# Loading the first expert's rows behind raw weights, splitting its weights without VectorE, and mixing its first products into the last head pair's order

## The chip, the cores and the metric

The kernel runs on one core of one Trainium2 chip. The time is device microseconds from start to end of one execution; a kernel's time is the median of its runs. Engines are called PE (TensorE), DVE (VectorE), ACT (ScalarE), POOL (GpSimd) and SP (SyncE, which here only issues transfers and loads registers). Each engine works through its own instructions in program order.

## The reference

Bucketed attention on 4 batches, 8 heads, 768 tokens and head size 64, and then a mixture of 8 experts on the 3072 tokens:

```
q_bucket, k_bucket = bits of sign(q @ proj), sign(k @ proj)      # 6 bits
scores = q @ k^T / 8, minus 1e9 where the buckets differ
attn   = softmax(scores) @ v                                     # x: 3072 x 512
expert = argmax(x @ w_gate); gate = softmax(x @ w_gate)[expert]
out    = gate * (relu(x_e @ w1[e]) @ w2[e])                      # per expert e
```

## The kernel before, in words

The attention part runs over 16 groups of one pair of heads each. A pair has 12 units (128 rows by 768 keys of one head). The order of each pair's work is written out by hand as a string of words: `HEAD` for the first pair, `PLAN` for the middle ones, `LAST` for the last pair. Every engine receives its instructions in the order in which the words are issued. A word with one or two dashes works for the pair before or the one before that. The words of `LAST` are:

- `S` score products of a unit (PE, L297 and L299), `R` their row minimum (DVE, L307), `X` the exponential (ACT, L313).
- `T` four transposes of the exponentials (PE, L327), `E..a` or `E..v` their copy out of PSUM on ACT (L379) or DVE (L377). `V0` and `V1` are the products with the values for the first and second half of the rows (PE, 24 matmuls, L389), `O` their copy on ACT (L395).
- `K` the product of the attention output with the router's weights and an identity (PE, L409), `L` its scaled copy (DVE, L419). `M` inverts the row sums.
- `n` and `t` are the two halves of one weight part of the first expert: a copy that rounds the raw weights (`nP` on POOL, `nA` on ACT) and the subtraction that leaves the rest (`tP` on POOL, `tV` on DVE, L964). There are 16 parts: 0 to 7 for the first matrix, 8 to 15 for the second. Eight parts are done at such words, the others by `weights` behind an `R` of an odd unit, copy and subtraction both on POOL (L714, L715). Two raw buffers hold two parts each; finishing an odd part issues the next raw load (L704, on SP).
- `r0` and `r1` are single steps of the generator `route_last` (L492) for the two halves of the last batch's last rows. Its first step takes a PSUM tile of the two named `t`, the third step ends with an exponential on ACT (L515), the fourth is a count on PE (L480, L482), the fifth and sixth give the slots and the gate on DVE (L522 to L530). `c0` and `c1` write these rows to DRAM at their slots, three indirect transfers each on POOL (L539).
- `x`, `g`, `h` turn the first expert's rows (transposes on PE L801, copy on ACT L803, rest on DVE L805). They read `XG[0]`, which `rows(0)` loads from DRAM (L744). `m` is one of eight products of the first matrix (12 matmuls on PE, L822), `u` its relu on ACT (L836), `d` the rest on DVE (L838). `m4` to `m7` need parts 4 to 7, `m0` to `m3` parts 0 to 3.

PSUM has two tiles named `t` (used by T, V, K and the routing steps) and three named `s` (used by S, x, m and the second products). A tile can be taken again when its last reader, in program order, is done.

Behind the last word, `rows(1)` loads the second half of the first expert's rows (L744); it reads rows that `c0` and `c1` have written, so it waits on SP for them. Then `rank_all` orders the experts and SP reads seven registers (L601), and only then come the raw loads for the second expert. PE goes on with the two second products of the first rows (48 matmuls, L879); four of the transposes of `rows(1)` stand behind the 44th of them (L784). After that come the first products of the second half, whose relu copies on ACT alternate with the second expert's weight copies.

In the last pair `route_step` writes the first half of an earlier batch's rows at the first three `R` words, and issues `rows(0)` at the third.

Of the kernel before, what the change touches and what calls it, by code (L numbers as in the profile page):

```python
# [31 lines left out]
M0 = float(2 ** 34)  # L32
# [22 lines left out]
def lsh_attention_moe(ctx, tc, qk, qk2, v, proj, wg, w1, w1p, w2, out):  # L55
# [634 lines left out]
    def raw_load(c, a):  # L690

        r, k = divmod(c, 4)
        if k < 2:
            src = (w1p if r else w1)[bass.ds(EV[r], 1)].rearrange("o (a p) f -> p (o a) f", p=128)[:, 2 * a:2 * a + 2,
                                                                                k * 512:(k + 1) * 512]
        else:
            o = (k - 2) * 4 + 2 * a
            src = w2[bass.ds(EV[r], 1)].rearrange("o (a p) d -> p (o a) d", p=128)[:, o:o + 2, :]
        n = 2 * c + a
        if n < 10 or n % 2:  # L700
            t = moe.tile([128, 2, 512], F32, name="raw", bufs=2)
        else:
            t = P2["p"].tile([128, 2, 512], F32, name="raw2", bufs=2)
        nc.sync.dma_start(t, src)  # L704
        RAW[c, a] = t
# [21 lines left out]
    def rows(n):  # L727

        r, o, c = PH[n]
        if n >= 2:  # L730
            b = -(-c // 32)
            x = XB[n] = P2["p"].tile([128, CB, 4 * 32], F32, name="xb")
            for a in range(4):
                nc.sync.dma_start(x[32 * a:32 * a + 32, :b],
                                  xsv[bass.ds(EV[r], 1), o:o + 32 * b, a * PW + E:a * PW + E + 2 * D]
                                  .rearrange("o (b i) w -> i (o b) w", i=32))
            t = len(tiles_of(c))
            XG[n] = P2["p"].tile([128, 4, 2], F32, name="xg", bufs=2)
            nc.sync.dma_start(XG[n][:, :t], xsv[bass.ds(EV[r], 1), o:o + 128 * t, GC:GC + 2]
                              .rearrange("o (j p) w -> p (o j) w", p=128))  # L740
            return
        XG[n] = wk.tile([128, 2, RW], F32, name="xd")
        for j, (i, _) in enumerate(tiles_of(c)):
            nc.sync.dma_start(XG[n][:, j], xsv[bass.ds(EV[r], 1), o + i:o + i + 128].rearrange("o p w -> p (o w)"))  # L744
# [190 lines left out]
    NC = NU // 2  # L935
    routes, parts, pick = {}, list(range(16)), pick_first()

    def weights(n):

        for _ in range(n):  # L940
            k = parts.pop(0)
            chunk_part(k // 4, k % 4)
            h = k // 2 + 2
            if k % 2 and h < 8:
                raw_load(h // 2, h % 2)

    def weight_half(op, x):

        if op == "n":
            k = parts.pop(0)  # L950
            c, a = divmod(k, 4)
            if a == 0:
                CH[c] = moe.tile([128, 2, 4, 512], F32R, name=HOME[c])
            o, i = CH[c][:, 0, a], RAW[c, a // 2][:, a % 2]
            if x == "A":
                nc.scalar.activation(o, i, AF.Copy)
            else:
                nc.gpsimd.tensor_copy(o, i)
            lows.append(k)
        else:  # L960
            k = lows.pop(0)
            c, a = divmod(k, 4)
            w, r = CH[c], RAW[c, a // 2][:, a % 2]
            ENG[x].tensor_tensor(w[:, 1, a], r, w[:, 0, a], op=OP.subtract)  # L964
            h = k // 2 + 2
            if k % 2 and h < 8:
                raw_load(h // 2, h % 2)
# [15 lines left out]
    """.split()  # L983

    LAST = """
        S5 R5 nP T30- E30a- S1 nP T31- E31v- S4 X5 nP T32- E32v- S0 R0 X0 K0-- L0-- R4 X4 tV V1- S8 tP O1- tP R1 X1
        M1- T21 E21v T20 E20a S2 R2 T01 E01a T22 E22a X2 S6 R6 X6 K1- L1- T00 E00v S11 R11 X11 S3 M0- T02 E02v R3 X3
        V0- O0- R8 X8 S10 T11 E11v T10 E10a S7 nP tP S9 M0 T12 R10 E12a X10 V0 R9 X9 O0 T40 E40a T51 E51a T41 E41a T42
        R7 E42a T50 E50a T52 E52v K0 L0 nP tV x0 X7 T31 E31a T30 T32 E30a M1 E32v K0- g0 h0 V1 O1 K1 nP tP nA tP L0-
        r0 r0 r0 r0 r0 r0 c0 x2 g2 h2 m6 u6 m1 u1 L1 r1 r1 r1 r1 r1 d6 r1 c1 d1 m7 u7 d7 m3 u3 d3 m4 u4 d4 m2 u2 d2 m0  # L990
        u0 d0 nP tP m5 u5 d5
    """.split()

    SCAT = {}
# [8 lines left out]
    def route_step(g, w, k):  # L1003

        b, q = divmod(g - NP, NP)
        if 0 <= b < B - 1 and w[0] == "R" and q == 1 and {(g - 2, "L0"), (g - 2, "L1")} <= DONE and steps[b] < 6:
            if b not in routes:
                routes[b] = route(b)
            on(b, 1)
        if 0 <= b < B - 1 and q == 2:  # L1010
            if w == "G":
                on(b, 8 - steps[b])
            elif w[0] == "R" and 8 <= steps[b] < 11:
                on(b, 1)
        s = {7: (0, 0), 8: (0, 1), 11: (1, 0), 12: (1, 1), 14: (2, 0)}.get(g)
        if w == "P7" and s:
            go(scatter(*s), 4)
        if g == NG - 1 and w[0] == "R" and k < 3:
            if k == 0:
                SCAT[0] = scatter(2, 1)  # L1020
            go(SCAT[0], 1)
            if k == 2:
                rows(0)

    def loads(g):

# [26 lines left out]
    def step(g, w):  # L1053

        n = g - w.count("-")
        w = w.rstrip("-")
        if w[0] in "SRXTEVOMKLDGHPBNA":
            z = n, w.rstrip("av")
            if n < 0 or z in DONE:
                return  # L1060
            DONE.add(z)
        op, x = w[0], w[1:]
        if op == "S":
            i = 12 * n + int(x)
            if i % 2 == 0:
                before(i // 2)
            score(i)
        elif op == "R":
            i = 12 * n + int(x)
            peak(i)  # L1070
            behind(i)
        elif op == "X":
            expo(12 * n + int(x))
        elif op == "T":
            trans(6 * n + int(x[0]), int(x[1]))
        elif op == "I":
            loads(n)
        elif op == "D" and n:
            blocks(12 * n + int(x))
        elif op == "E":  # L1080
            trans_ev(6 * n + int(x[0]), int(x[1]), x[2] == "v")
        elif op == "V":
            for kt in range(NT):
                pv(2 * n + int(x[0]), kt)
        elif op == "O":
            pv_end(2 * n + int(x))
        elif op == "M":
            sums(2 * n + int(x))
        elif op == "K":
            TK[2 * n + int(x)] = tok(2 * n + int(x))  # L1090
        elif op == "L":
            tok_ev(2 * n + int(x), TK.pop(2 * n + int(x)))
        elif op == "G" and n + 1 < NG:
            lsh_mm(n + 1)
        elif op == "H" and n + 1 < NG:
            lsh_ev(n + 1)
        elif op == "B" and 0 < n < NG - 1:
            lsh_bits(n + 1)
        elif op == "N" and n + 1 < NG:
            mask(2 * n + 2)  # L1100
            mask(2 * n + 3)
        elif op == "A" and n + 1 < NG:
            if x == "2":
                xk = XL[n + 1][:, S:]
                nc.gpsimd.tensor_scalar(xk, xk, KS, 1.0, op0=OP.mult, op1=OP.mult)
            else:
                upper(2 * n + 2, int(x))
        elif op == "P" and n + 1 < NG:
            split(2 * n + 2 + int(x) // 4, int(x) % 4)
        elif op in "kjqlp":  # L1110
            cut(op, int(x[0]), int(x[1]), x[2])
        elif op == "y":
            lsh_first(int(x[0]), int(x[1]))
        elif op == "b":
            bits_first(int(x[0]), int(x[1]))
        elif op == "f":
            if x == "0":
                before(0)
            score(0, (x == "1",))
        elif op == "i":  # L1120
            if int(x[0]) not in SC:
                SC[int(x[0])] = ps.tile([128, 2, 512], F32, name="s", bufs=3)
            warmth(SC[int(x[0])][:, 0], int(x[1]))
        elif op == "s":
            split(2 + int(x[0]), int(x[1]))
        elif op == "z":
            mask(2 + int(x))
        elif op == "w":
            lsh_bits(1)
        elif op in "xgh":  # L1130
            xt_first(op, int(x))
        elif op == "m":
            mm1(0, int(x))
        elif op in "ud":
            relu(op, int(x))
        elif op == "r":
            go(last[int(x)], 1)
        elif op == "c":
            go(scatter(B - 1, int(x)), 4)
        elif op in "nt":  # L1140
            weight_half(op, x)

    last = [route_last(B - 1, 0), route_last(B - 1, 1)]
    for g in range(NG):
# [146 lines left out]
```

## Time and profile before

| | |
|---|---|
| median of 3 runs | 710.57 us (710.15 to 710.75) |
| the profiled execution | 709.86 us, of which the span is 708.1 us |
| PE busy | 694.2 us, 98% of the span, 4219 matmuls |
| DVE, ACT, POOL busy | 446.7, 433.6, 470.7 us |
| TensorE clock granted, mean | 0.995 of full speed |

The attention part takes the first 400 us, the experts the rest. PE's busy share says how long a matmul was in it, not that it ran at its full rate: a matmul that runs at half clock is twice as long and counts as busy. So the slices of PE's share must be read beside the granted clock.

### The profile page before, as it was taken

The numbers are of one execution on the slowest core, as the hardware profiler recorded it, in microseconds if no ns is written. First come the engines' busy times: TensorE is split into PE (matmuls) and PEld (weight loads), VectorE is DVE, ScalarE is ACT, GpSimd is POOL, SyncE is SP. The second block draws the span as 40 slices with busy tenths as digits, with TensorE's granted clock in tenths as the row PEclk, the third lists the DMA queues.
The fourth block names the chain that finished last, engine by engine and source line by source line (L and its number), as shares of the span: only waits on it lengthen the run. The fifth ranks groups of instructions, "written<-read, shape, count | busy, mean of one in ns | idle before, by whom it ended". The sixth has DMA issues, their size and how long they took to land.

```text
span 708.1 us, 12282 instructions
## 1 busy us (share of the span) xinstructions
PE 694.2 (98%) x4219; PEld 566.5 (80%) x4219; DVE 446.7 (63%) x916; ACT 433.6 (61%) x863; POOL 470.7 (66%) x520
## 2 busy tenths in 40 slices
PE   8999999999999999999999799999999999999997
PEld 5777777776877686867776589899999999989896
DVE  8878787878787778788882533541838533362521
ACT  7988888878888788887865114644344344444320
POOL 7967755695785967867938335765667676768532
PEclk9999999999999999999999899999999999999999
DMA  7519777885977556875693138476446394738101
GB/s 288 151 38 263 202 220 204 245 232 184 272 218 213 160 148 200 223 221 150 197 275 111 68 131 243 164 194 145 157 135 172 123 183 148 194 134 223 70 10 41
DMA packets 64528, 123.09 MB, mean 174 GB/s; under 512 B 15329, under 2 KB 29025, under 8 KB 64400
## 3 DMA queue, kind: packets, MB, share of 16 engines
q1 hardware_dynamic: 56736, 103.17, 51.6%
q0 software_dynamic: 7584, 19.10, 8.5%
q8 instruction: 34, 0.56, 0.4%
q14 instruction: 30, 0.25, 0.1%
q10 hardware_dynamic: 144, 0.02, 0.0%
HBM read 65.75 MB, written 26.33 MB: 130 GB/s over the span
## 4 chain that ended last, share of the span: by engine, by line
PE 90%; issue 4%; POOL 2%; ACT 1%; DVE 1%; DMA 0%; POOLq 0%; ACTq 0%
PE t L389 19%; PE s L822 18%; PE s L859 10%; PE s L297 10%; PE s L299 9%; PE t L327 9%; PE s L879 8%; PE t L409 3%; PE t L254 2%; PE s L888 1%; POOL w L718 1%; PE t L103 1%; POOL w L715 0%; ACT e L313 0%; DMA out_dram<-e,ix 0%
## 5 line engine op out<-in xcount | busy, mean ns | idle before, releaser
L307 DVE TENSOR_SCALAR_CACHE_REDUCE e<-s 128x768 f32<-128x768 f32 x192 | 178.7, 953 | 61.4 <-PE s L299 52.4
L313 ACT ACTIVATE e<-e,m 128x768 f32<-128x768 f32 x192 | 178.0, 930 | 15.2 <-DVE e L307 12.9
L718 POOL TENSOR_TENSOR w<-raw,w 128x512 fp32r<-128x512 f32 x112 | 144.4, 1315 | 38.6 <-ACT w L717 37.9
L389 PE MATMUL t<-pt,vt 128*64 128x384 f32 x768 | 133.7, 499 | 2.8 <-DVE pt L377 2.8
L822 PE MATMUL s<-xh,w 128*128 128x456 f32 (+6 forms) x672 | 126.8, 346 | 0.0
L822 PEld LDWEIGHTS s<-xh,w 128*128 128x128 f32 x672 | 119.2, 188 | 3.0
L389 PEld LDWEIGHTS t<-pt,vt 128*64 128x64 f32 x768 | 53.4, 139 | 68.4 <-issue 63.4
L838 DVE SCALAR_TENSOR_TENSOR hh<-s,hh 128x256 fp32r<-128x256 f32 (+7 forms) x64 | 35.5, 555 | 109.2 <-ACT hh L836 109.1
L327 PE MATMUL t<-ident,e 128*128 128x128 f32 x648 | 92.0, 274 | 1.3 <-DVE pt L377 0.5
L379 ACT ACTIVATE pt<-t 128x512 f32<-128x512 f32 (+1 forms) x148 | 82.3, 581 | 13.7 <-PE t L327 12.3
L836 ACT ACTIVATE hh<-s 128x256 fp32r<-128x256 f32 (+7 forms) x64 | 31.3, 490 | 90.3 <-PE s L822 86.9
L327 PEld LDWEIGHTS t<-ident,e 128*128 128x128 f32 x648 | 76.7, 140 | 8.1 <-ACT pt L379 1.9
L349 DVE STREAM_TRANSPOSE w<-e 128x768 f32<-128x768 f32 x84 | 79.1, 964 | 0.8 <-DMA pt<-w 0.6
L859 PE MATMUL s<-hh,w 128*128 128x456 f32 (+3 forms) x384 | 74.9, 356 | 0.0
L859 PEld LDWEIGHTS s<-hh,w 128*128 128x128 f32 x384 | 71.1, 188 | 2.6
L717 ACT ACTIVATE w<-raw 128x512 fp32r<-128x512 f32 x112 | 66.4, 622 | 3.3 <-DMA raw<-in_w1p_dram 3.3
L895 POOL DMA_INDIRECT out_dram<-y,ix x26 | 25.9, 995 | 62.0 <-DVE y L893 29.4
L879 PE MATMUL s<-w,hh 128*128 128x512 f32 (+1 forms) x240 | 56.4, 394 | 0.0
L297 PE MATMUL s<-w 80*128 80x384 f32 x192 | 55.3, 369 | 0.0
L297 PE MATMUL s<-qk 80*128 80x384 f32 x192 | 54.9, 368 | 0.0
L879 PEld LDWEIGHTS s<-w,hh 128*128 128x128 f32 (+1 forms) x240 | 44.7, 187 | 10.4
L299 PE MATMUL s<-qk 128*128 128x384 f32 x192 | 49.8, 341 | 0.0
(219 smaller groups left out, 987.1 us busy)
## 6 DMA issues: line engine op xcount, KB each, us to landing
pt<-w SPq DMA_DIRECT2D x224, 144.0 KB, 3.7
raw<-in_w_dram SPq DMA_DIRECT2D x36, 512.0 KB, 3.4
raw<-in_w1p_dram SPq DMA_DIRECT2D x28, 512.0 KB, 3.3
xd<-in_qk_dram SPq DMA_DIRECT2D x14, 768.0 KB, 7.7
sorted_rows<-xr SPq DMA_DIRECT2D x6, 1156.0 KB, 7.8
vt<-in_v_dram SPq DMA_DIRECT2D x16, 384.0 KB, 3.4
masks<-bits POOLq DMA_DIRECT2D x14, 192.0 KB, 4.0
sorted_rows<-sorted_rows SPq DMA_DIRECT2D x2, 1156.0 KB, 6.1
```

Source lines behind the costliest of these rows:

```text
L297: nc.tensor.matmul(p[:, a, :HALF], k[0:80, 2, c], k[0:80, 3, n], start=i >= 4, stop=i < 4)
L299: nc.tensor.matmul(p[:, a, :HALF], k[:, 0, c], k[:, 1, n], start=i < 4, stop=i >= 4)
L307: nc.vector.tensor_scalar(e, SC.pop(i)[:, :, :HALF], CEIL, None, op0=OP.min, op1=OP.min, accum_out=m)
L313: nc.scalar.activation(e, e, AF.Exp, bias=m, scale=-1.0, accum_out=SM[g, hf][:, t, s:s + 1])
L327: nc.tensor.transpose(o[:, j, w], e[w][:, kt // 3, (kt % 3) * 128:(kt % 3) * 128 + 128], ident)
L349: nc.vector.transpose(z[:, :, c, w].rearrange("p g (k i) -> p g k i", i=32), e)
L379: nc.scalar.activation(o, x, AF.Copy)
L389: nc.tensor.matmul(p[s * 64:(s + 1) * 64, :HALF], VT[g][:, kt, s, :], PT[u][:, :, :, s, kt].rearrange("p a t i -> p t a i"), start=(kt == ...
L718: nc.gpsimd.tensor_tensor(w[:, 1, a], r, w[:, 0, a], op=OP.subtract)
L822: nc.tensor.matmul(p[:, :c], w[:, a, d, fs], x[:, b, d, :c], start=(k == 0), stop=(k == 11))
L859: nc.tensor.matmul(p[:, :c], w[:, a, f % 4, ms], h[b][:, f, :c], start=(k == 0), stop=(k == 23))
L879: nc.tensor.matmul(p[:pw], HH[n][b][:, f, i:i + pw], w[:, a, f % 4], start=(k == 0), stop=(k == 23))
```

## The change

Four edits. `rows(0)` is no longer issued at the third `R` word but as soon as four of the sixteen parts have been taken (behind the raw load that this part issues). No weight part has its subtraction on DVE or its copy on ACT any more; nine parts go through `nP` and `tP`. The order of the words of `LAST` is another: of the eight products `m` of the first expert three stand between the transposes of the last pair, one between them and `V1`, one between `V1` and `K1`, and three behind that; `x2`, `x0` come ahead of the last scores. And eviction copies have changed engines here and there.

```
+    def rows_asked():
+        if len(parts) <= 12 and 0 not in XG:
+            rows(0)
 ...
             if k % 2 and h < 8:
                 raw_load(h // 2, h % 2)
+            rows_asked()
 ...
     LAST = """
-        S5 R5 nP T30- E30a- S1 nP T31- E31v- S4 X5 nP T32- E32v- S0 R0 X0 K0-- L0-- R4 X4 tV V1- S8 tP O1- tP R1 X1
-        M1- T21 E21v T20 E20a S2 R2 T01 E01a T22 E22a X2 S6 R6 X6 K1- L1- T00 E00v S11 R11 X11 S3 M0- T02 E02v R3 X3
-        V0- O0- R8 X8 S10 T11 E11v T10 E10a S7 nP tP S9 M0 T12 R10 E12a X10 V0 R9 X9 O0 T40 E40a T51 E51a T41 E41a T42
-        R7 E42a T50 E50a T52 E52v K0 L0 nP tV x0 X7 T31 E31a T30 T32 E30a M1 E32v K0- g0 h0 V1 O1 K1 nP tP nA tP L0-
-        r0 r0 r0 r0 r0 r0 c0 x2 g2 h2 m6 u6 m1 u1 L1 r1 r1 r1 r1 r1 d6 r1 c1 d1 m7 u7 d7 m3 u3 d3 m4 u4 d4 m2 u2 d2 m0
-        u0 d0 nP tP m5 u5 d5
+        S5 nP tP R5 T31- E31a- S1 T30- E30v- S0 R0 X5 T32- E32a- K0-- L0-- X0 S8 R8 X8 nP tP M1- R1 X1 V1- O1- S4 R4
+        T00 E00a T01 E01v S6 T02 E02v R6 S3 R3 X4 T21 E21a T20 E20a S2 S11 X6 T22 R2 X2 E22a R11 V0- O0- x2 g2 h2 x0
+        g0 h0 K1- L1- S7 S9 X3 M0 T11 T10 E11a E10v M0- S10 nP tP X11 K0- L0- nP tP nP tP nP tP nP tP nP tP T12 R10 R9
+        E12a V0 X9 X10 T51 O0 T50 m4 E50v T52 R7 E51a T40 u4 d4 m7 E52a E40a T41 E41v T42 E42v m5 X7 M1 T31 E31a T30
+        E30a T32 K0 L0 r0 r0 r0 u5 d5 m2 u7 d7 E32a V1 O1 u2 d2 m3 u3 d3 r0 K1 L1 r1 r1 r1 r0 r0 c0 m1 u1 d1 m0 u0 d0
+        m6 u6 d6 r1 r1 r1 c1
     """.split()
 ...
             go(SCAT[0], 1)
-            if k == 2:
-                rows(0)
 ...
             weight_half(op, x)
+            if op == "t":
+                rows_asked()
```

## Rows read from the trace of the kernel before

**Rows 1.** Chain that ended last, in order of time: start us, us, engine, tile, line, count.

```profile
365.77 0.73 PE t L409 x6
368.80 4.09 PE t L389 x24
373.79 0.87 PE t L327 x8
376.51 4.04 PE t L389 x24
405.34 8.73 PE s L822 x72
414.07 10.26 PE s L879 x44
```

**Rows 2.** Timeline of PE: start us, us, line, operation, count [idle before <-releaser].

```profile
380.47 4.00 PE L327 MATMUL t<-ident,e 128*128 128x128 f32 x24
391.32 6.92 PE L389 MATMUL t<-pt,vt 128*64 128x384 f32 x24 [2.77 <-DVE pt L377]
398.89 1.00 PE L409 MATMUL t<-wgt,ot 128*128 128x144 f32 x6 [0.65 <-ACT ot L395]
424.17 0.60 PE L784 MATMUL t<-ident,xd 128*128 128x128 f32 x4
```

**Rows 3.** Stretches of 2 us: busy time by engine, granted clock, DMA share, GB/s.

```profile
388.00:390.00 2.00, 0.55 (x5) 0.33 (x3) 0.66 (x1) 0.00 (x0) 1.92 (x4) 1.00 0.05 15
390.00:392.00 2.00, 0.68 (x2) 0.29 (x4) 1.97 (x6) 0.00 (x0) 1.52 (x1) 0.56 0.71 247
392.00:394.00 2.00, 2.00 (x10) 0.78 (x8) 0.38 (x1) 0.00 (x0) 0.00 (x0) 0.50 0.00 0
396.00:398.00 2.00, 2.00 (x12) 0.61 (x8) 0.00 (x0) 0.00 (x0) 0.00 (x0) 0.73 0.00 0
```

**Rows 4.** Timeline of DVE, the same columns.

```profile
389.34 1.06 DVE L964 TENSOR_TENSOR w<-raw,w 128x512 fp32r<-128x512 f32 x1 [3.19 <-POOL w L958]
390.61 0.65 DVE L377 COPY pt<-t 128x512 f32<-128x512 f32 x1
400.95 0.17 DVE L522 TENSOR_TENSOR pb<-t,pb 128x8 f32<-128x8 f32 x1 [0.36 <-PE t L482]
401.90 0.18 DVE L530 RECIPROCAL xr<-rf 128x3 f32<-128x3 f32 x1
402.67 0.60 DVE L419 TENSOR_TENSOR xr<-t,r 128x432 f32<-128x432 f32 x1
404.86 0.18 DVE L514 TENSOR_TENSOR rl<-t,rf 128x24 f32<-128x24 f32 x1
```

**Rows 5.** Timeline of ACT, the same columns.

```profile
387.38 0.60 ACT L803 ACTIVATE xhe<-s 128x512 fp32r<-128x512 f32 x1
400.62 0.22 ACT L515 ACTIVATE ex<-rl 128x24 f32<-128x24 f32 x1 [1.26 <-DVE rl L514]
```

**Rows 6.** Timeline of POOL, the same columns.

```profile
402.85 1.01 POOL L539 DMA_INDIRECT sorted_rows<-xr,slot  x1 [2.00 <-issue]
410.05 0.96 POOL L539 DMA_INDIRECT sorted_rows<-xr,slot  x1 [0.21 <-issue]
```

**Rows 7.** Timeline of SP's issues, the same columns; `x16` spans sixteen issues.

```profile
353.60 12.55 SPq L355 DMA_DIRECT2D pt<-w  x16
366.65 0.90 SPq L744 DMA_DIRECT2D xd<-sorted_rows  x2
413.74 0.90 SPq L744 DMA_DIRECT2D xd<-sorted_rows  x2
421.58 8.57 SPq L704 DMA_DIRECT2D raw<-in_w1p_dram  x3
```

**Rows 8.** Issues of the DMA view: KB each, median us from issue to landing.

```profile
pt<-w SPq DMA_DIRECT2D x224, 144.0 KB, 3.7
xd<-sorted_rows SPq DMA_DIRECT2D x4, 289.0 KB, 2.7
```

## The prediction

> **What bounds the kernel now.** PE is busy 98% of the span, so I looked for the stretch where it isn't, or where it isn't at full rate. Three views, in this order. The chain of waits, read for what one step costs when nothing holds it: `K` 0.73 us, eight transposes (two `T`) 0.87, a `V` 4.04, 72 of the 96 matmuls of the first expert's `m` 8.73 [rows 1]. Then PE's timeline over the end of the last pair, where the same steps cost more: six `T` take 4.00 us instead of 2.61, `V1` starts 2.77 us after PE has gone idle and then takes 6.92, and the last `K1` waits 0.65 [rows 2]. Then the granted clock in stretches of 2 us: 1.00 through the idle time, falling within 390 to 392, 0.50 until between 396 and 398 [rows 3]. `V1` ran at the lower level of 1.2 GHz, which cost 6.95 - 4.04 = 2.9 us [rows 1, 2].
>
> Why `V1` waited is in DVE's timeline: the eviction of the last transposes (L377 at 390.61) stood behind a weight subtraction (L964) that had held DVE for 3.19 us, because POOL had not made that part's copy [rows 4].
>
> How much is there in all? From `V0` (376.51) to the second products (414.07) PE takes 37.6 us [rows 1]. The work in it at full rate: two `V` 8.1, six `T` 2.6, three more 1.3, three `K` 2.2, `x0` and `x2` 0.9, the eight `m` 96/72 x 8.73 = 11.6, the two counts 0.3; together 27.0. So 10.6 us are waiting and low clock. The matmuls are the same after the change; only this excess can go.
>
> **What the change takes away.** All 10.6 us of that excess stand at places that it rebuilds. DVE no longer stands behind a weight part, so the 2.77 us in front of `V1` lose their cause; the transposes get `m`s between them. The nine parts that now go `nP tP`, and all others, are POOL's alone; POOL was idle for long before, and its parts come due well ahead of their `m`s and second products. I cost them at nothing; POOL's own loads cover it, and if that cover goes, `m4` waits.
>
> **What it adds: four waits on PE.**
>
> First, `V0-` now stands ahead of `K1-`, which was ahead of it. Its operand comes by sixteen transfers, the last of them issued by about 365.5 (353.60 + 12.55, less one issue of 0.6) with a median landing of 3.7 us [rows 7, 8]; `V0-` began at 368.80 [rows 1]. PE is there one `K` earlier, 0.7 us, and waits that long if the transfers don't come sooner. Bounds 0 and 0.8; I take 0.7.
>
> `x2` follows directly. `rows(0)` was issued at 366.65 as soon as SP had done those sixteen transfers, ahead of two raw loads [rows 7]; now the two raw loads go first, some 1.2 us of issuing, and the rows are issued at about 367.9. With the median landing of 2.7 us [rows 8] they are there at 371.2 (the second at 368.5 + 2.7), and PE comes to `x2` when `V0-` ends, at 368.8 + 4.1 = 372.9. I take 0. What speaks against this part of the change: the Trainium skill (DMA: Bandwidth & Descriptors, Queues, rings and completion order) says that one issuing engine's transfers are taken in the order of its ring on each DMA engine, so that the rows would come after 1 MB of weights. No row of mine shows the landing of rows behind weights; by that rule `x2` would wait perhaps half a microsecond, as an estimate, and the sum would be that much higher. The sum doesn't include it.
>
> Small waits between evictions and transposes, of the kind that cost 4.00 - 2.61 = 1.4 us for six `T` [rows 1, 2]: most of the new `T` have an `m` or an `S` beside them, but `T12`-`V0` and `T30`-`T32`-`K0` stand alone. Bounds 0.3 and 1.4; I take 1.0.
>
> Then `V1` again. It needs one of the two PSUM tiles `t`. One was taken by the first step of `r0`, which holds it to its fifth; the other holds the transposes of `T32` until `E32a` has copied them. In the new order ACT does `E32a` behind the exponential of the third `r0`, `u5` and `u7`, and that exponential waits for `K0`, `L0` and the router's chain on DVE. From the start of `K0`: 1.0 us to its end (the last `K1`) [rows 2], from `L0` to the end of L514 2.37 (402.67 to 405.04) [rows 4], the exponential 0.2 [rows 5], `u5` and `u7` 0.3 each, `E32a` 0.6 (an ACT copy of that size) [rows 5], hand-overs 0.1: 4.8 us. PE has `K0` (0.73) and `m2` (1.46) to do: 2.2. It stands still for **2.6 us**. DVE's stall on a weight part has been replaced by ACT's on the router. Behind the waiting exponential on ACT are queued exactly the two relus and the eviction that PE needs. Bounds 2.2 and 3.0.
>
> So up to the second products: 10.6 taken away, 0.7 + 1.0 + 2.6 = 4.3 added; they begin 6.3 us earlier at full clock.
>
> The fourth is `rows(1)`. The last scatter `c1` has moved to the end of the order, and POOL does six indirect transfers in a row, first `c0`, which waits for `r0`'s gate. From the start of `K1`: 1.0 to its end, `L1` and three `r1` steps 2.4, the last steps of `r0` 1.1 (400.95 to 402.08) [rows 4], 0.8 to POOL's first indirect transfer (402.08 to 402.85), 7.2 from that to the last one (402.85 to 410.05, of which some 0.6 was a wait for `r1`'s gate that falls away, so 6.6) [rows 4, 6], 3.7 until SP issues `rows(1)` (413.74), 0.5 to its second transfer and 2.7 to its landing [rows 6 to 8]: 18.8 us. PE from the same point: `K1` 0.7, three `m` 4.4, the count 0.1, and 44 matmuls of the second products 10.3 [rows 1]: 15.5. Before, the rows landed about 417.0 and PE asked for them at 424.17 [rows 2]; now PE asks first and waits **3.3 us**. Of the 6.3 us 3.0 are left. Bounds 2.5 and 4.0. Behind `rows(1)` on SP stand seven register loads and the raw loads for the second expert (7.8 us after it before, 413.74 to 421.58 [rows 7]); the copies on ACT that use them now alternate with relus that PE waits for. 0 to 1 us; I take 0.4 for it. That leaves 2.6.
>
> **The clock.** The one time that PE stood still for 2.77 us here, the granted clock fell to the lower level and `V1` lost 2.9 us [rows 2, 3]. Now there are two such gaps, of 2.6 and of 3.3 us. If `V1` falls again, its 2.9 us are spent as before. Behind the second gap stand the transposes and the first products of the second half; no row shows a fall there, so between 0 and 2.9 again. Part of that stretch is waiting for copies on ACT and DVE in any case, where a slow PE costs nothing, so I take half, 1.4. Together 4.3 us.
>
> **Sum.** -2.6 + 4.3 = +1.7 us. On the profiled execution (709.86 us, of which 708.1 are the span) this gives 711.6; that execution lies 0.7 below the median of 710.57, and against the median it gives 712.3.
>
> **The rivals.** *Only one of the gaps lowers the clock*: for it speaks that the first gap is a little shorter than 2.77 and follows a full-rate `m2`, against it that the fall before came before the gap was over. -2.6 + 2.9, or -2.6 + 1.4: 709.4 to 710.9, say 710.2. *Neither does*: this is the other side, faster. The place is the 2.6 us ahead of `V1` and the 3.3 ahead of L784; it decides if the granted clock stays 1.00 in both; price 4.3 us; 708.0. *The scatter's chain is hidden*: if POOL's indirect transfers run closer than 1.3 us apart or `rows(1)` needs only its own half, PE doesn't wait at L784, has no second gap either, and about 6 us stay less the clock of `V1`: 707.2. *The rows of the first half come late*: if two raw loads of 0.5 MB go wholly ahead of them and they land at 375 or later, PE stands at `x2` for some 2.5 us more, which shifts everything behind it: 714.8. *The change doesn't do what it says*, so that the products can't start among the transposes because weights aren't there: `m4` then waits on POOL and nothing is won, 711 to 713.
>
> **How the numbers follow.** Forecast (both gaps lower the clock) 0.50, one only 0.23, neither 0.09, scatter hidden 0.07, rows late 0.07, no effect 0.04. A measurement of this kernel tells 0.2%, 1.4 us, from no change: below 709.1 is faster, above 712.0 slower. Of the forecast (its own range 710.6 to 714.0) I count 0.38 slower and 0.12 the same; of the second case 0.20 the same and 0.03 faster; the third and fourth faster; the fifth slower; the last half and half. Faster 0.19, same 0.34, slower 0.47. The range leaves out the far ends of the fourth and fifth: 708.0 to 714.8.
>
> **What would show it.** In the profile after: no L964 on DVE and no idle time of DVE for POOL; `V1` waiting 2 to 3 us with ACT's L379 as the releaser and, on ACT, L515 just before L836, L836 and L379; the second products starting 3 to 6 us earlier than 414; then a gap of PE of 2.5 to 4 us in front of L784, with SP's L744 issued after 416; the granted clock at 0.50 behind both gaps. Wrong would be a `V1` that starts right behind `m2`, or rows that are there when L784 asks. If the clock falls behind neither gap, the kernel is faster and my sum is off by its last term.

## The result, and the profile after

The changed kernel takes 713.64 us (median of 17 runs, 710.84 to 715.97) against 709.87 us for the kernel before (17 runs measured beside it, 707.22 to 711.95). The ratio is 1.0055, with a 95% interval of 1.0042 to 1.0069: 3.9 us slower by the ratio, 3.8 by the medians. The forecast was 1.7 us slower, with a range of 708.0 to 714.8.

The profiled execution took 715.26 us, with a span of 713.5 us against 708.1 before. It lies 1.6 us above the median of its runs, and its mean granted clock of 0.992 is the lowest among them, so what the lower clock costs is read here at its upper end. PE's timeline over the stretch of [rows 2], after the change (start us, us, engine, line, operation, count [idle before <-releaser]):

```profile
353.16 0.62 PE L297 MATMUL s<-w 80*128 80x384 f32 x2
369.35 4.09 PE L389 MATMUL t<-pt,vt 128*64 128x384 f32 x24 [0.68 <-DMA pt<-w]
373.65 0.30 PE L801 MATMUL s<-ident,xd 128*128 128x128 f32 x1 [0.21 <-DMA xd<-sorted_rows]
374.28 0.98 PE L801 MATMUL s<-ident,xd 128*128 128x128 f32 x7 [0.34 <-DMA xd<-sorted_rows]
398.22 5.79 PE L389 MATMUL t<-pt,vt 128*64 128x384 f32 x24 [2.38 <-ACT pt L379]
410.82 10.52 PE L879 MATMUL s<-w,qk 128*128 128x512 f32 x44
423.77 0.33 PE L784 MATMUL t<-ident,xd 128*128 128x128 f32 x1 [2.43 <-DMA xd<-sorted_rows]
424.46 0.55 PE L784 MATMUL t<-ident,xd 128*128 128x128 f32 x3 [0.36 <-DMA xd<-sorted_rows]
426.25 4.61 PE L822 MATMUL s<-xhe,w 128*128 128x256 f32 x36
433.46 10.14 PE L822 MATMUL s<-xhe,w 128*128 128x256 f32 x60 [2.61 <-DVE hh L838]
```

The last pair begins at 353.16; in the profile before it began at 352.55. Nothing of PE's work ahead of that point was changed, so I take these 0.6 us for a difference between executions. The second products begin at 410.82, 3.1 us sooner than before (413.91 or 414.07 by the view) in spite of the later beginning [rows 1]. At L784 it is 0.4 us sooner (423.77 against 424.17) [rows 2], and where the first products of the second half begin it is level (426.25 against 426.07). Then the order turns: the fourth product of the second half begins at 433.46, where the kernel before had it at 430.82, and the last sixty matmuls of that group take 10.14 us instead of 7.45. So all of this execution's loss stands behind 426.25.

There are three large gaps, of 2.38 us ahead of `V1`, 2.43 (and 0.36) ahead of L784, and 2.61 ahead of the fourth product of the second half. The stretches around the first and the third, in columns as in [rows 3]:

```profile
396.00:398.00 2.00, 0.00 (x0) 0.00 (x0) 1.34 (x7) 1.09 (x4) 0.00 (x0) 1.00 0.00 0
398.00:400.00 2.00, 1.78 (x8) 0.81 (x10) 0.19 (x1) 0.17 (x1) 0.00 (x0) 0.66 0.03 8
400.00:402.00 2.00, 2.00 (x10) 0.79 (x8) 0.00 (x0) 0.00 (x0) 0.00 (x0) 0.50 0.00 0
402.00:404.00 2.00, 2.00 (x13) 0.64 (x9) 0.00 (x0) 0.00 (x0) 0.00 (x0) 0.98 0.00 0
432.00:434.00 2.00, 0.54 (x2) 0.54 (x3) 0.65 (x2) 1.43 (x4) 0.45 (x1) 0.70 0.24 59
434.00:436.00 2.00, 2.00 (x12) 2.00 (x11) 0.62 (x2) 1.05 (x3) 2.00 (x2) 0.50 1.11 336
```

The granted clock falls to 0.50 (1.2 GHz) behind the first gap and behind the third. Behind the second it stays at 1.00.

Who keeps PE waiting each time is in the timelines of the other engines. ACT, then POOL, then SP:

```profile
396.91 0.22 ACT L515 ACTIVATE ex<-rl 128x24 f32<-128x24 f32 x1 [3.56 <-DVE rl L514]
397.04 0.64 ACT L836 ACTIVATE qk<-s 128x256 fp32r<-128x256 f32 x2
397.57 0.60 ACT L379 ACTIVATE pt<-t 128x512 f32<-128x512 f32 x1
432.57 0.38 ACT L836 ACTIVATE hh<-s 128x256 fp32r<-128x256 f32 x1 [5.65 <-DMA out_dram<-e,ix]
```

```profile
410.78 1.01 POOL L539 DMA_INDIRECT sorted_rows<-xr,slot  x1 [15.92 <-issue]
417.39 0.97 POOL L539 DMA_INDIRECT sorted_rows<-xr,slot  x1 [0.21 <-issue]
427.02 0.99 POOL L895 DMA_INDIRECT out_dram<-e,ix  x1 [7.30 <-DVE e L893]
```

```profile
366.98 1.01 SPq L704 DMA_DIRECT2D raw<-in_w_dram  x2
368.44 0.90 SPq L744 DMA_DIRECT2D xd<-sorted_rows  x2
420.82 0.90 SPq L744 DMA_DIRECT2D xd<-sorted_rows  x2
426.02 6.62 SPq L704 DMA_DIRECT2D raw<-in_w1p_dram  x3
```

First gap: ACT stands 3.56 us at the router's exponential (L515), then does two relus and only then the eviction (L379 at 397.57) for which `V1` waits. Second gap: POOL's six indirect transfers run from 410.78 to 417.39, and `rows(1)` is issued at 420.82, 7.1 us later than before [rows 7]. Third gap: the first relu of the second half waits for the output rows that POOL sent at 427.02, and starts at 432.57, 5.55 us after they were sent; in the kernel before it was 3.15 us (426.78 to 429.93). (The relu writes a tile `hh` that is made after the attention's tiles have been given back, and the output rows are sent from one of those.) The raw loads for the second expert, 4.4 us later than before (426.02 against 421.58) [rows 7], now start 1.0 us ahead of that sending instead of 5.2. POOL, ACT and PE at the same place in the kernel before:

```profile
426.78 0.98 POOL L895 DMA_INDIRECT out_dram<-e,ix  x1 [4.61 <-DVE e L893]
429.93 0.38 ACT L836 ACTIVATE hh<-s 128x256 fp32r<-128x256 f32 x1 [3.19 <-DMA out_dram<-e,ix]
426.07 4.59 PE L822 MATMUL s<-xhe,w 128*128 128x256 f32 x36
430.82 7.45 PE L822 MATMUL s<-xhe,w 128*128 128x256 f32 x60 [0.16 <-DVE hh L838]
```

### The profile page after: what moved, and what is told of

Same layout as the page of the kernel before. It is cut to its first block, busy times and chain, and to the rows that moved or that the text cites. A ratio compares the mean times of both kernels' runs of the same rounds, so it can differ in the third digit from the quotient of the medians.

```text
span 713.5 us, 12272 instructions
## 1 busy us (share of the span) xinstructions
PE 695.0 (97%) x4219; PEld 568.6 (80%) x4219; DVE 443.2 (62%) x913; ACT 433.2 (61%) x863; POOL 474.6 (67%) x523
## 4 chain that ended last, share of the span: by engine, by line
PE 81%; issue 9%; POOL 3%; DMA 3%; SPq 2%; ACT 1%; DVE 1%; POOLq 0%; ACTq 0%; DVEq 0%
PE s L822 17%; PE t L389 16%; PE s L859 10%; PE s L297 9%; PE s L299 9%; PE t L327 8%; PE s L879 6%; PE t L409 3%; SPq L355 2%; PE t L254 2%; DMA raw<-in_w_dram 1%; PE s L888 1%; POOL w L718 1%; DMA out_dram<-e,ix 1%; DMA xd<-in_qk_dram 1%
## 5 line engine op out<-in xcount | busy, mean ns | idle before, releaser
L379 ACT ACTIVATE pt<-t 128x512 f32<-128x512 f32 (+1 forms) x149 | 82.9, 582 | 17.4 <-PE t L327 15.6
```

What stands on the lines that cost most here:

```text
L379: nc.scalar.activation(o, x, AF.Copy)
```

## The experiments

My theory from here on: the two small edits (rows later, no weights on VectorE) are gains, and the loss comes from three places of the new order, the exponential ahead of `E32a` on ACT, the late row of scatters on POOL, and raw loads that run beside the output rows; the clock makes gaps dearer. The rivals: the rows that wait behind raw weights, or POOL with all the weights, cost the time; or the gaps are one wait that only moves when it is closed at one place.

Ratios are to the kernel before, measured beside it on the same chip, with 95% intervals.

**The eviction first.** In the changed kernel `E32a` is issued ahead of `r0`.

```
- E30a T32 K0 L0 r0 r0 r0 u5 d5 m2 u7 d7 E32a V1 O1
+ E30a T32 E32a K0 L0 r0 r0 r0 u5 d5 m2 u7 d7 V1 O1
```

> The changed kernel with one word moved: E32a, the last eviction that V1 needs, stands ahead of the router's steps r0 in the order, so ACT does it before the exponential that waits for the router. My theory (ACT was held by the router's chain): V1 starts right behind m2, its 2.4 us of waiting go, the granted clock stays 1.00 and V1 takes 4.1 us instead of 5.8; everything behind it, the scatter's chain too, moves by the same 4.1 us; about 709.5 us, from 708.5 to 710.5. Rival (the loss in front of V1 is only a symptom, because PE meets the rows of the second half anyway): the 4 us turn up as a longer wait at L784, about 713.5 us.

Measured: 709.87 us, ratio 1.0001 (0.9984 to 1.0017); 3.8 us under the changed kernel. PE's timeline:

```profile
393.47 1.68 PE L822 MATMUL s<-xhe,w 128*128 128x256 f32 x12
395.08 4.09 PE L389 MATMUL t<-pt,vt 128*64 128x384 f32 x24
419.40 0.33 PE L784 MATMUL t<-ident,xd 128*128 128x128 f32 x1 [2.90 <-DMA xd<-sorted_rows]
430.07 8.94 PE L822 MATMUL s<-xhe,w 128*128 128x256 f32 x60 [2.20 <-DVE hh L838]
```

`V1` follows `m2` without a gap and takes 4.09 us. The other two gaps are there as before, 2.90 and 2.20, so the gain isn't waited for elsewhere: the scatters move with `V1`. The order on ACT is shown as the cause of the first gap. In this execution the granted clock fell behind the gap at L784 too (columns as in [rows 3]), and the fall behind the third gap cost less, 8.94 us for the sixty matmuls instead of 10.14:

```profile
420.00:422.00 2.00, 1.92 (x7) 1.51 (x8) 0.99 (x4) 0.66 (x2) 0.00 (x0) 0.64 0.04 8
422.00:424.00 2.00, 2.00 (x10) 1.91 (x9) 1.58 (x3) 0.77 (x2) 0.64 (x1) 0.50 0.66 189
```

**The scatters earlier.** The last steps of `r0` with `c0`, and of `r1` with `c1`, are issued sooner.

```
- E32a V1 O1 u2 d2 m3 u3 d3 r0 K1 L1 r1 r1 r1 r0 r0 c0 m1 u1 d1 m0 u0 d0 m6 u6 d6 r1 r1 r1 c1
+ E32a r0 V1 O1 r0 r0 c0 u2 d2 m3 u3 d3 K1 L1 r1 r1 r1 m1 u1 d1 r1 r1 r1 c1 m0 u0 d0 m6 u6 d6
```

> The changed kernel with the last steps of r0 and its scatter c0 moved ahead of m3, and the last steps of r1 and c1 moved ahead of m0 and m6. My theory (six indirect transfers in a row on POOL set the time of rows(1)): the last indirect transfer starts near 414 instead of 417.4, rows(1) is issued near 417.5 and PE no longer waits 2.4 and 0.4 us at L784; about 710.8 us if the wait of 2.6 us at the relu of the second half stays, down to 706 if that goes too. Rival (rows(1) waits for something else, or what is won there is waited for at the relu): 713 us or more.

Measured: 708.71 us, ratio 0.9981 (0.9962 to 0.9999); 4.9 us under the changed kernel.

```profile
397.91 5.79 PE L389 MATMUL t<-pt,vt 128*64 128x384 f32 x24 [1.03 <-ACT pt L379]
421.85 0.60 PE L784 MATMUL t<-ident,xd 128*128 128x128 f32 x4
430.64 7.46 PE L822 MATMUL s<-xhe,w 128*128 128x256 f32 x60 [2.35 <-DVE hh L838]
```

L784 no longer waits, so POOL's row of scatters was what set it. The third gap has stayed, 2.35 us, but in this execution the clock didn't fall behind it (7.46 us), which accounts for the rest of the gain; that part need not be the scatters' own.

**Smaller raw loads.** The first two loads for the second expert bring an eighth of the columns.

```
+        if c == 4:
+            nc.vector.memset(t, 0.0)
+            nc.sync.dma_start(t[:, :, :64], src[:, :, :64])
+        else:
             nc.sync.dma_start(t, src)
```

> The changed kernel with the first two raw loads of the second expert cut to an eighth of their columns, the rest set to zero on DVE; seven eighths of half of that expert's first matrix are left out. Theory (the wait of 2.6 us in front of the fourth product of the second half comes from the output rows of the first half, whose landing took 5.5 us instead of 3.1 because the raw loads now run at the same time): the landing is near 3 us again, that wait shrinks to 0.2 us or less, the clock doesn't fall behind it; about 5 us less, 708.5 us, from 707.5 to 710. Rival (the landing is slow by itself, or the relu waits for the weight copies on ACT): 713 us.

Measured: 710.14 us, ratio 1.0006 (0.9990 to 1.0022); 3.5 us under the changed kernel and just outside what I expected (707.5 to 710). POOL, ACT and PE of this kernel (four lines were added to it, so L840 and L826 are the relu and the product):

```profile
426.94 0.98 POOL L899 DMA_INDIRECT out_dram<-e,ix  x1 [7.20 <-DVE e L897]
430.32 0.38 ACT L840 ACTIVATE hh<-s 128x256 fp32r<-128x256 f32 x1 [3.48 <-DMA out_dram<-e,ix]
431.21 7.45 PE L826 MATMUL s<-xhe,w 128*128 128x256 f32 x60 [0.42 <-DVE hh L842]
```

From sending to the relu it is 3.4 us again instead of 5.55, the gap is 0.42, and the clock stays up (7.45 us). The raw loads beside the output rows are the cause of the third gap. Two other runs, which load all columns, fit: with the raw loads issued 1.8 us ahead of the output rows (eviction first) it is 5.8 us, and with them 6.1 us ahead (ranking first, below) 3.3 us. And without the third gap the change is no loss: 1.0006.

**Fillers.** Is `V1` slow because the clock fell? Ten dummy matmuls ahead of it should keep PE busy. The first form put them into a PSUM tile of their own.

> The changed kernel with ten dummy matmuls of 512 bf16 columns between m2 and V1, into a PSUM tile that nobody reads, so that PE is busy for 2.2 us of the 2.4 that it waits there. V1 starts when it did. Theory (V1 is slow because the clock falls after the gap): V1 takes 4.1 us instead of 5.8 and the kernel 1.7 us less, about 711.9 us, from 711 to 712.8. Rival (V1 is slow for another reason, its operands or the traffic): 713.6 us or more.

Measured: 714.36 us, ratio 1.0057 (1.0037 to 1.0078), no gain. The fillers waited themselves:

```profile
398.43 4.00 PE L103 MATMUL s<-ones 128*128 128x512 bf16 x10 [2.10 <-DVE qk L838]
402.36 4.09 PE L389 MATMUL t<-pt,vt 128*64 128x384 f32 x24
```

All three tiles were in use, so they started only when `d7`, behind the exponential too, had freed one, and ran at the lower clock themselves. The second form wrote into the unused half of `m2`'s tile.

```
+        FILL2[n, f] = p[:, 1]                    # mm1: tile of two banks, the second unused
- r0 r0 r0 u5 d5 m2 u7 d7 E32a V1
+ r0 r0 r0 u5 d5 m2 W u7 d7 E32a V1              # W: ten matmuls into FILL2[0, 2]
```

> The changed kernel with ten dummy matmuls of 512 bf16 columns right behind m2, into the half of m2's PSUM tile that nobody reads, so that they wait for nothing and PE is busy for 2.2 of the 2.4 us that it waits ahead of V1. V1 starts when it did. Theory (V1 is slow because the clock falls after the gap): V1 takes 4.1 us instead of 5.8 and the kernel 1.7 us less, about 711.9 us, from 711 to 712.8. Rival (V1 is slow for another reason): V1 still takes 5.8 us, 713.6 us.

Measured: 711.53 us, ratio 1.0024 (1.0010 to 1.0039); 2.1 us under the changed kernel.

```profile
395.34 2.33 PE L103 MATMUL s<-ones 128*128 128x512 bf16 x10
397.89 4.09 PE L389 MATMUL t<-pt,vt 128*64 128x384 f32 x24 [0.22 <-ACT pt L379]
```

`V1` starts when it did (397.89 against 398.22) and takes 4.09 us instead of 5.79: the idle time ahead of it, not its operands, made it slow. These 1.7 us are read directly; the kernel's 2.1 us are not the same 1.7, because behind `V1` this execution differs too (a gap of 3.25 us at L784 with the lower clock behind it, and a third gap of 1.31).

**One part alone: the rows.** The kernel before with `rows_asked` in place of the call in `route_step`, nothing else.

> The kernel before with one edit of the change alone: the rows of the first half are loaded behind the second and third raw loads. Theory (the raw loads were what held POOL, and POOL's copy held DVE in front of V1): raw weights land 2.6 us sooner (370.9 instead of 373.5), POOL's copy of the part that DVE subtracts is there before DVE asks, the gap of 2.8 us ahead of V1 closes to under 1 us and the clock doesn't fall; about 705 us, from 704 to 707, so this part is a gain of 4 to 5 us. Rival (the order of loads is hidden either way): 709.9 us.

Measured: 705.07 us, ratio 0.9938 (0.9919 to 0.9957). POOL's copy of part 4, first in the kernel before and then in this one; and of this one DVE's subtraction and eviction, and PE's `V1`:

```profile
373.45 0.61 POOL L714 CAST w<-raw 128x512 fp32r<-128x512 f32 x1 [12.11 <-DMA raw<-in_w_dram]
```

```profile
370.56 0.61 POOL L714 CAST w<-raw 128x512 fp32r<-128x512 f32 x1 [8.92 <-DMA xd<-sorted_rows]
```

```profile
386.53 1.06 DVE L970 TENSOR_TENSOR w<-raw,w 128x512 fp32r<-128x512 f32 x1 [0.19 <-POOL w L964]
387.95 0.69 DVE L377 COPY pt<-t 128x512 f32<-128x512 f32 x1
```

```profile
388.69 4.09 PE L389 MATMUL t<-pt,vt 128*64 128x384 f32 x24
```

POOL starts this part 2.9 us sooner. (The profile puts the end of its wait down to the rows' transfer, which ran beside that of the weights.) DVE's wait for POOL is 0.19 us instead of 3.19 [rows 4], and `V1` follows the product ahead of it with no gap and at the full clock [rows 2]. Loading the rows behind raw weights is worth some 4.4 us by itself: not for the rows, for the weights. (In the old order the same edit puts the rows behind one raw load, issued at 366.75, and ahead of the others; in the changed kernel two go first.)

**One part alone: no weights on VectorE.** The kernel before with `tP` for `tV` and `nP` for `nA`.

> The kernel before with one edit of the change alone: the words tV and nA of its order are tP and nP, so no weight part is on DVE or ACT. Theory (the wait ahead of V1 was DVE's on POOL): the eviction of the last transposes follows them at once, V1 starts near 388.4 instead of 391.3 and runs at 4.1 us, 5.9 us less in all, about 704 us, from 703 to 706. Rival (POOL, with two more subtractions, becomes the bound, and the products wait for its parts): 709 us or more.

Measured: 704.50 us, ratio 0.9928 (0.9909 to 0.9947). `V1` again follows at once (389.61, 4.09 us). POOL didn't become the bound.

**Both parts, the old order.**

> The kernel before with the edits for the rows and for the weight parts together and its own order of words kept: all of the change but the new order. Theory (both edits remove the same wait ahead of V1): 704 to 705 us, no better than the better of the two alone, and 9 us less than the changed kernel, so that the whole loss is the new order's. Rival (each has a gain of its own): 700 us.

Measured: 705.38 us, ratio 0.9938 (0.9920 to 0.9956). The two edits close the same wait, and together they bring what each brings alone. The changed kernel is this one with the new order: 1.0055 against 0.9938, so the order alone costs 1.2%, some 8 us.

**Both moves in the changed kernel,** and then the ranking ahead of `rows(1)` as well.

```
-    rows(1)
     rank_all()
+    rows(1)
```

> The changed kernel with both moves together: E32a ahead of r0, and the last steps of r0, c0, r1 and c1 earlier. If the two waits are separate, their gains of 3.8 and 4.9 us add: about 705 us, from 704 to 707. If the one covers the other: 708.5 us, like the better of the two alone. The wait at the relu of the second half (2.4 us) stays in either case.

> As the run before it, and with the ranking of the experts issued ahead of rows(1), so that SP reads its seven registers while it would wait for the scatter. Theory (the relu of the second half waits for output rows that land beside the raw loads): the raw loads start 4 us sooner, right behind rows(1), and are through when the output rows are written; their landing is near 3 us, the wait at the relu under 0.5 us: 2 to 5 us less than the run before it, 701 to 703.5 us. Rival (the raw loads now delay the rows of the second half instead, and PE waits at L784): no gain over the run before it.

Measured: 707.14 us, ratio 0.9968 (0.9948 to 0.9988), and 707.06 us, ratio 0.9960 (0.9947 to 0.9973). The two moves bring 6.5 us together where 3.8 and 4.9 alone add to 8.7; with both, PE still waits 1.10 us for a router step (L514) ahead of `V1`, where the eviction alone left no gap. With the ranking first I had expected 2 to 5 us more; the rival's figure, no gain, was right. The first kernel's gap at the relu and its issue of `rows(1)`, and then the second's issue and PE:

```profile
428.63 7.46 PE L822 MATMUL s<-xhe,w 128*128 128x256 f32 x60 [1.55 <-DVE hh L838]
416.14 0.90 SPq L744 DMA_DIRECT2D xd<-sorted_rows  x2
```

```profile
417.50 0.92 SPq L744 DMA_DIRECT2D xd<-sorted_rows  x2
420.74 0.30 PE L784 MATMUL t<-ident,xd 128*128 128x128 f32 x1 [0.83 <-DMA xd<-sorted_rows]
422.19 0.55 PE L784 MATMUL t<-ident,xd 128*128 128x128 f32 x3 [1.15 <-DMA xd<-sorted_rows]
424.19 12.98 PE L822 MATMUL s<-xhe,w 128*128 128x256 f32 x96
```

The relu no longer waits (96 matmuls in one piece), but now PE waits 0.83 and 1.15 us for the rows of the second half. Two things delay them, and the rival names only the second. SP reads the seven registers first, so `rows(1)` is issued 5.8 us after the last scatter began (411.69) instead of 3.6 (412.59 in the kernel with the two moves alone). And the raw loads run beside the rows: the first transpose starts 3.2 us after the issue and the others 4.7, where in the changed kernel it was 3.0 and 3.6. The granted clock fell behind these gaps as well (0.50 from 424 to 426), and the 96 matmuls took 12.98 us. How the missing gain divides between the three isn't shown.

**A product ahead of `K1` in the old order.**

```
- E32v K0- g0 h0 V1 O1 K1 nP tP nP tP L0- r0 r0 r0 r0 r0 r0 c0 x2 g2 h2 m6 u6 m1 u1 L1
+ E32v K0- x2 g0 h0 g2 h2 V1 O1 m6 u6 K1 nP tP nP tP L0- r0 r0 r0 r0 r0 r0 c0 m1 u1 L1
```

> As the run before it, with one product of the first expert (m6, and x2, g2, h2 which it needs) moved ahead of K1, where PE waits 0.65 us for the copy of V1's result, and with that 0.3 us ahead of m6 covered too. Theory (what the new order wanted can be had without its waits): 1 to 1.5 us less than the run before it, near 703 us. Rival (DVE, which now turns the rows ahead of the router's steps, makes the router later): no gain.

Measured: 705.99 us, ratio 0.9940 (0.9921 to 0.9958): no gain; the rival was right. The waits of 0.65, 0.74 and 0.28 us around `K1` are gone, and a later one has come:

```profile
399.54 0.19 PE L480 MATMUL t<-ohs,tri 128*128 128x32 bf16 x1 [1.93 <-DVE rl L514]
```

The four kernels with the old order and one or both small edits are the fastest of all that ran, and beat both the kernel before and the changed one; among the four (0.9928 to 0.9940) the intervals tell no order. The new order with both moves (0.9968) stays some 2 us behind them, though its interval touches three of theirs: PE's waits of 1.10 us ahead of `V1`, 1.05 ahead of the second count and 1.55 at the relu are left in it, and no run closed all three. What the changed engines of the eviction copies are worth was not tried by itself.

## Why the prediction was right, and where it was not

The sign was right, and so were the waits at `V1` and L784 with what causes them; the size was too small, 1.7 us forecast and 3.9 measured, and the sign came out in part by luck. Where the first products of the second half begin, the changed kernel was level with the kernel before (426.25 against 426.07, or 0.4 us ahead without its later start). The loss stands behind that, in a third wait and the lower clock after it, for which I had 0.4 us and another cause. Of the 1.7 us of my own sum, 1.4 were for a fall of the clock behind L784, which this execution doesn't show. With the third gap all but closed the kernel took 710.14 us, ratio 1.0006: the time of my second case (710.2), in which one gap only lowers the clock.

- *The excess that goes.* The second products were to begin 6.3 us earlier at full clock, 3.4 with `V1` at the lower one. They began 3.1 us earlier, 3.7 without the later start of that execution; with the 1.7 us of `V1`'s clock added back, 5.4 at full clock. The waits that the timeline lists up to there are 4.1 us against my 4.3, so some 1.1 us of the excess did not go.
- *`V0-`*: 0.7 expected, 0.68 measured.
- *`x2`*: 0 expected, 0.55 measured (0.21 and 0.34). The rows were issued at 368.44 and PE could go on at 373.65, 5.2 us later, not 2.7 as in [rows 8]. The Trainium skill (DMA: Bandwidth & Descriptors, Queues, rings and completion order) says that each DMA engine takes a ring's descriptors in order. The trace agrees: the DMA engines were busy for 0.97 of the time from 372 to 373 us and for 0.11 from 373 to 374, and the rows, issued last, could be used at 373.65. I had named it and left it out of the sum.
- *Small waits at the transposes*: 1.0 expected; the timeline lists 0.26 ahead of `V0` and 0.25 ahead of `T32`.
- *POOL's weight parts*: nothing expected, and `m4` begins (385.52) without a listed wait. They are eight at the words of the order, not nine, as many as before.
- *`V1`'s wait*: 2.6 expected from the chain on DVE and ACT, 2.38 measured, with the releaser and the order on ACT as forecast.
- *`rows(1)`*: 3.3 expected, 2.8 measured (2.43 and 0.36), with SP's issue at 420.82.
- *`V1`'s clock*: 2.9 expected, 1.7 measured (5.79 against 4.09). The fall came some 0.4 us after `V1` began (a mean of 0.66 over 398 to 400 is 0.64 us at 1.00 and the rest at 0.50) and not 1 us ahead of it, as the mean of 0.56 over 390 to 392 gives for the kernel before [rows 3].
- *What failed* is the term behind `rows(1)`: "0 to 1 us; I take 0.4". It measured 2.6, where the kernel before had 0.16. I had looked at the copies on ACT that need the raw weights. What met the raw loads instead was another transfer, the output rows of the first half, on whose landing the first relu of the second half depends. The Trainium skill (DMA: Bandwidth & Descriptors, Issuing engines are not separate DMA queues) says that transfers from SP and POOL share the same DMA engines and interleave; the 5.55 us beside the loads and 3.4 us with an eighth of them agree. I had the issue of the raw loads in [rows 7] and moved it in time, but asked only who waits for it, not what it runs beside.
- *The second fall of the clock*: 1.4 expected behind L784. In this execution it didn't come there, but behind the third gap, and cost 2.7 (10.14 against 7.45). In the executions with a longer wait at L784 (2.90 us with the eviction first, 2.70 and 3.25 with the fillers) it did come there.

What the change takes away was also argued too narrowly. I had counted the order of the rows and raw loads only as a cost at `x2`, and taken it at 0. Alone it is a gain of 4.4 us, because the earlier raw weights let POOL run ahead of DVE. In my forecast both small edits stood behind the same removed wait, which is right for the sum; only the parts alone show that either would have been enough, and that the new order gives back all of it and 4 us more.

Whether the gaps' cost differs from run to run only through the clock isn't settled. It fits that the 17 runs of the changed kernel spread over 5 us and that the execution of 715.97 us had a mean granted clock of 0.992 while those of 710.84 and 711.15 had 0.996 and 0.999, but the executions also differ by some tenths of a microsecond ahead of the changed code. The kernel before doesn't lose clock in every execution either: of the 17 measured beside the kernel with both parts in the old order, three with a mean granted clock of 0.999 took 707.38 to 707.97 us, the others, at 0.994 to 0.996, 708.88 to 712.03.

## What to carry to other kernels

When work is woven into an order written by hand, follow each engine's own queue: a short instruction that waits for a long chain (here an exponential for the router) holds every eviction behind it, and the engine that matters waits for those. A chain that runs over POOL's indirect transfers, DRAM and back should be started as early as its inputs allow; moving it to the end of the order puts its whole length in front of the next stage. And when a transfer moves in time, ask not only who waits for it but which other transfer will now run beside it. Try the edits of a change one by one: here two of them were worth 5 us, and the new order took 8.

## What the runs showed of the hardware

The indirect write of 128 output rows needed 3.15 us from sending to the relu that waits for it with 1 MB of weight loads issued 5.2 us earlier, 5.55 us with the loads issued 1.0 us earlier, and 3.4 us with an eighth of them at that time. Six indirect transfers in a row on POOL started 1.3 to 1.5 us apart, 6.6 us from the first to the last (410.78 to 417.39).

Gaps of PE of nearly the same length did not cost the same. 2.38 us ahead of `V1` and 2.61 us ahead of the fourth product were followed by a granted clock of 0.50; 2.43 and 0.36 us ahead of L784 were not, in the same execution; 2.90 us there, with the eviction first, were. With the scatters earlier two gaps, of 1.11 and 1.03 us, close together ahead of `V1` were followed by the lower clock (5.79 us), and a gap of 2.35 us later was not; with both moves one gap of 1.10 us ahead of `V1` was not (4.09 us). The cost of such a gap is best taken as a range from nothing to 2.9 us on top of its length.
